# Top-k attention with a leaky-ReLU MLP: the weights of the last units of five chunks transposed on TensorE

## The chip, the cores and the metric

The kernel runs on one core of a Trainium2 chip. The metric is device time in microseconds (us): the median of three runs is 1514.51 us, and they lie between 1513.94 and 1515.4. The profile is of one further execution, with a span of 1512.7 us from the first to the last instruction.

Names of the engines in the profile: PE is TensorE (PEld its loading of weights), DVE is VectorE, ACT is ScalarE, POOL is GpSimd, SP is SyncE, which issues the DMAs.

## What is computed

An attention that keeps 32 scores of each row, and then an MLP with a leaky ReLU:

```python
# q, k, v: (8, 8, 576, 64) float32
scores = scale * np.matmul(q, k.transpose(0, 1, 3, 2))
kth = np.partition(scores, -32, axis=-1)[..., -32:-32 + 1]
scores = np.where(scores >= kth, scores, -1000000000.0)
scores = scores - np.max(scores, axis=-1, keepdims=True)
attn = np.exp(scores)
attn = attn / (np.sum(attn, axis=-1, keepdims=True) + 1e-09)
o = np.matmul(attn, v)
# (B, H, S, D) -> (B*S, H*D): 4608 tokens of 512
x = o.transpose(0, 2, 1, 3).reshape(4608, 512)
h = x @ w_in                      # w_in (512, 2048)
g = np.maximum(0.01 * h, h)
out = g @ w_out                   # w_out (2048, 512)
```

## The kernel before

The weights of the MLP come as 64-bit numbers in 16 pieces and are rounded to float32 on the chip in a first stage of some 80 us. Then the kernel works through 144 units. A unit is 128 query rows of a pair of heads, and step s does parts of several units: the top-k of unit s on VectorE, the mask of unit s-1 on GpSimd and its exponents on ScalarE, and the normalizing and transposing of unit s-2. In even steps come the scores of two units and the products with the values of two units. Tokens are gathered in chunks, two of 128 and then 17 of 256; when all units of a chunk have their values, the MLP of the chunk may run, and its matmuls are dealt out over the following steps.

The program's order on each engine is that of this code; nothing is reordered. Each engine takes its instructions one after the other.

Rounding a piece (cut to what the change touches):

```python
nc.vector.tensor_scalar(scale, scale, 1151.0, 896.0, ALU.min, ALU.max)
if n % 2:
    nc.scalar.activation(scale, scale, AF.Copy, bias=-896.0 * 128, scale=128.0)     # L127
nc.vector.tensor_scalar(m_top, top, 0xF, 0x3F80, ALU.bitwise_and, ALU.bitwise_or)   # L128
nc.vector.tensor_scalar(top, top, 0x8000, None, ALU.bitwise_and)
if n % 2 == 0:
    nc.vector.tensor_scalar(scale, scale, 896.0, 128.0, ALU.subtract, ALU.mult)     # L131
# ... sums on TensorE into pw (in PSUM), then
nc.vector.tensor_tensor(scale, scale, top, ALU.bitwise_or)                          # L144
nc.vector.tensor_tensor(dst[:, at], pw, scale[:, at].bitcast(BF16), ALU.mult)       # L147
```

The parts of a unit's way that matter here:

```python
def exponents(u, i):                                   # L238
    nc.scalar.activation(u.s[i], u.s[i], AF.Exp, bias=u.nbias[:, i:i + 1], scale=SCALE,
                         accum_out=u.z[:, i:i + 1])

def sums(u):                                           # L243
    u.ze = small.tile([P, 2], F32, name="ze")
    nc.scalar.activation(u.ze, u.z, AF.Copy, bias=1e-9, scale=1.0)

def reciprocals(u):                                    # L247
    u.rz = small.tile([P, 2], F32, name="rz")
    nc.vector.reciprocal(u.rz, u.ze)

def normalize(u, i):                                   # L250
    nc.scalar.activation(u.s[i], u.s[i], AF.Copy, bias=0.0, scale=u.rz[:, i:i + 1])

def transpose(u):
    pairs = u.both.rearrange("p i n -> p (i n)").bitcast(U16).rearrange("p (n h) -> p n h", h=2)
    apart = halves.tile([P, 2, 2 * S], U16, name="apart")          # in DRAM
    for h in range(2):
        split = work.tile([P, 2 * S], U16, name="split", bufs=2)
        nc.scalar.copy(split, pairs[:, :, h])                      # L259
        nc.sync.dma_start(apart[:, h, :], split)
    u.wT = work.tile([P, 2 * NKC - 1, P], F32, name="wT", bufs=3)
    nc.sync.dma_start_transpose(out=u.wT.bitcast(U16), in_=apart.rearrange("p h n -> (p h) n"))
```

The budget that deals out the MLP. A step has seven slots; mlp_steps(budget) puts so many columns of matmul into the order, and the budget of a slot is what is left of the work that is ready, divided by the slots until the next chunk is ready:

```python
def values_at(n):
    return n + LAG + (n + LAG) % 2                     # LAG = 3: always an even step

def attended(s):
    for at, ch in ready_at:
        if at == s:
            ready.append(ch)
            backlog[0] += mlp_cost(ch)

def slot_budget(s):
    after = [at for at, _ in ready_at if at >= s]
    until = after[0] if after else s
    few = len(after) >= len(CHUNKS) - EARLY            # EARLY = 2
    return backlog[0] / (max(until + 1 - few - s, 1) * SLOTS)      # SLOTS = 7
```

And one step:

```python
cur, old, older = unit(s), unit(s - 1), unit(s - 2)
budget = slot_budget(s)
slot()                                 # a quarter of the top-k of cur, on VectorE
mask(old, 0); mask(old, 1)
mlp_steps(budget)
slot()
reciprocals(older); normalize(older, 0); normalize(older, 1)
mlp_steps(budget)
exponents(old, 0)
transpose(older)
slot()
mlp_steps(budget); mlp_steps(budget)
slot()
mlp_steps(budget)
exponents(old, 1)
sums(old)
# even steps: scores of one unit, values of two units, attended(s), scores of another
budget = slot_budget(s + 1)
mlp_steps(budget); mlp_steps(budget)
load_more(s)
```

The matmuls of the MLP are ph (first layer, L308 for the two small chunks and L333 for the others), evacuated by ScalarE into gT through the leaky ReLU (L313 and L339), and pz (second layer, L345). The small chunks have their activations transposed on TensorE (pt, L318, copied by L320). The scores are psc (L198), copied to s_sb (L207); the values are po (L283), copied to x (L297).

Of the kernel before, what the change touches and what calls it, by code (L numbers as in the profile page):

```python
# [8 lines left out]
F32 = mybir.dt.float32  # L9
# [4 lines left out]
ALU = mybir.AluOpType  # L14

NKC = 5
# [3 lines left out]
def kernel(  # L20
# [13 lines left out]
    nc = tc.nc  # L34
    NPAIR, P, S = qT.shape
# [24 lines left out]
    work = ctx.enter_context(tc.tile_pool(name="work", bufs=2))  # L60
# [3 lines left out]
    ps_po = ctx.enter_context(tc.tile_pool(name="ps_po", bufs=1, space=bass.MemoryType.PSUM))  # L64
    ps_ml = ctx.enter_context(tc.tile_pool(name="ps_ml", bufs=3, space=bass.MemoryType.PSUM))

    ident = const.tile([P, P], F32, name="ident")
# [12 lines left out]
    NPIECE = 2 * HP * DFF // WCH  # L80
# [3 lines left out]
    def piece(n):  # L84

        if n < NPIECE // 2:
            j, c = divmod(n, HP)
            return w_in[c][:, j * WCH:(j + 1) * WCH]
        f = 2 * (n - NPIECE // 2)
        return w_out[f // 4][:, f % 4:f % 4 + 2, :].rearrange("p g n -> p (g n)")  # L90
# [12 lines left out]
    def round_weights(n):  # L103

        raw = raw_of.pop(n)
        dst = piece(n)  # L110
        mid = raw[:, :, 2]
        low = raw.rearrange("p n w -> p (n w)").bitcast(U32).rearrange("p (n w) -> p n w", w=2)[:, :, 0]
        top = raws.tile([P, WCH], U16, name="top", bufs=2)
        scale = raws.tile([P, WCH], U16, name="scale", bufs=2)
        parts = work.tile([P, 2 * NKC - 1, P], F32, name="wT", bufs=3)
        parts = parts.rearrange("p c n -> p (c n)").bitcast(U16)
        m_top, m_low = parts[:, 0:WCH], parts[:, WCH:2 * WCH].bitcast(BF16)
        nc.scalar.copy(top, raw[:, :, 3])
        nc.scalar.activation(dst, mid, AF.Copy, bias=-7.0 - 2.0 ** -16, scale=2.0 ** -20)

        nc.scalar.activation(m_low, low, AF.Copy, bias=128.0, scale=2.0 ** -29)  # L121
        yield
        nc.vector.tensor_scalar(scale, top, 4, 0x7FF, ALU.logical_shift_right, ALU.bitwise_and)

        nc.vector.tensor_scalar(scale, scale, 1151.0, 896.0, ALU.min, ALU.max)
        if n % 2:
            nc.scalar.activation(scale, scale, AF.Copy, bias=-896.0 * 128, scale=128.0)  # L127
        nc.vector.tensor_scalar(m_top, top, 0xF, 0x3F80, ALU.bitwise_and, ALU.bitwise_or)  # L128
        nc.vector.tensor_scalar(top, top, 0x8000, None, ALU.bitwise_and)
        if n % 2 == 0:  # L130
            nc.vector.tensor_scalar(scale, scale, 896.0, 128.0, ALU.subtract, ALU.mult)  # L131
        if n < NPIECE - 3:
            pw = ps_sc.tile([P, 2, 512], F32, name=f"psc{n % 2}")
            sums = [(pw[:, h, :], h * 512) for h in range(2)]
            ends = [(pw.rearrange("p h n -> p (h n)"), 0)]
        else:
            ends = sums = [(ps_ml.tile([P, 512], F32, name="pw", tag="ml"), h * 512) for h in range(2)]
        for pw, c in sums:
            at = slice(c, c + 512)
            nc.tensor.matmul(pw, ident_top, m_top[:, at].bitcast(BF16), start=True, stop=False)  # L140
            nc.tensor.matmul(pw, ident, dst[:, at], start=False, stop=False)
            nc.tensor.matmul(pw, ident_low, m_low[:, at], start=False, stop=True)
        yield
        nc.vector.tensor_tensor(scale, scale, top, ALU.bitwise_or)  # L144
        for pw, c in ends:
            at = slice(c, c + pw.shape[-1])
            nc.vector.tensor_tensor(dst[:, at], pw, scale[:, at].bitcast(BF16), ALU.mult)  # L147
# [97 lines left out]
# [8 lines that stand above are left out]
# [8 lines left out]
        u.wT = work.tile([P, 2 * NKC - 1, P], F32, name="wT", bufs=3)  # L261
        nc.sync.dma_start_transpose(out=u.wT.bitcast(U16), in_=apart.rearrange("p h n -> (p h) n"))

    x_of = {}
# [89 lines left out]
    def mlp_cost(ch):  # L356
        n = CHUNKS[ch]
        if ch < EARLY:
            return NFC * DMODEL + NFC // 4 * (HP * 512 + 2 * P)
        return NFC * HP * max(n, 225) + -(-n // P) * NFC * DMODEL  # L360
# [4 lines left out]
    def mlp_steps(budget):  # L365
        owed[0] += budget
        while owed[0] > 0:
            if running[0] is None:
                if not ready:
                    owed[0] = 0.0  # L370
                    return
                running[0] = mlp(ready.pop(0))
            cost = next(running[0], None)
            if cost is None:
                running[0] = None
            else:
                owed[0] -= cost
                backlog[0] -= cost

    LAG = 3

    def values_at(n):

        return n + LAG + (n + LAG) % 2

    steps = units

    def unit(n):  # L390
        return steps[n] if 0 <= n < len(steps) else None
# [9 lines left out]
# [10 lines that stand above are left out]
        few = len(after) >= len(CHUNKS) - EARLY  # L411
        return backlog[0] / (max(until + 1 - few - s, 1) * SLOTS)
# [3 lines left out]
    with tc.manual_schedule():  # L416
        last = {p: n for n, u in enumerate(steps) for p in u.pairs}

        def load_more(s):

            for of, load, n, lag in ((qk_of, load_qk, LOADED, -2), (v_of, load_v, LOADED_V, LAG + 1)):
                while len(of) < NPAIR and (len(of) < n or last[len(of) - n] + lag <= s):
                    load(len(of))


        for n in range(3):
            load_weights(n)
        rounding = {}
        for n in range(NPIECE + 2):
            for i in (n, n - 1, n - 2) if AS_WORDS else ():  # L430
                if 0 <= i < NPIECE:
                    if i == n:
                        rounding[i] = round_weights(i)
                    next(rounding[i], None)
            load_weights(n + 3)
            if 6 <= n < 6 + HP:
                load_qk(n - 6)
            elif n == NPIECE - 1:
                for u in steps[0:2]:
                    scores(u)  # L440
            if n == NPIECE - 1:
                load_v(0)
                load_v(1)

        for s in range(len(steps) + LAG + 1):
            cur, old, older, new = unit(s), unit(s - 1), unit(s - 2), ()
            if s % 2 == 0:
                new = [u for u in steps[s + 2:s + 4] if u]
            picks = top_k(cur) if cur else iter(())
            budget = slot_budget(s)  # L450

            def slot():
                next(picks, None)

            slot()
            if old:
                mask(old, 0)
                mask(old, 1)
            mlp_steps(budget)
            slot()  # L460
            if older:
                reciprocals(older)
                normalize(older, 0)
                normalize(older, 1)
            mlp_steps(budget)
            if old:
                exponents(old, 0)
            if older:
                transpose(older)
            slot()  # L470
            mlp_steps(budget)
# [3 lines that stand above are left out]
            if old:  # L475
                exponents(old, 1)
                sums(old)
            for u in new[:1]:
                scores(u)
            if s % 2 == 0:  # L480
                po = ps_po.tile([P, 2, P], F32, name="po")
                for values in (weigh_values, keep_values):
                    for n, u in enumerate((unit(s - LAG - 1), unit(s - LAG))):
                        if u:
                            values(u, po[:, n, :])
                attended(s)
            for u in new[1:]:
                scores(u)
            budget = slot_budget(s + 1)
# [3 lines that stand above are left out]
        mlp_steps(1e9)  # L493
# [58 lines left out]
```

## Time and profile before

| | before |
|---|---|
| time, median of 3 | 1514.51 us |
| span of the profile | 1512.7 us |
| PE busy | 1429.0 us (94%) |
| PE loading weights | 934.5 us (62%) |
| DVE busy | 1330.4 us (88%) |
| ACT busy | 1121.5 us (74%) |
| POOL busy | 1079.5 us (71%) |
| DMA of the kernel's queue | 225.49 MB, 54.2% of 16 engines |
| mean granted TensorE clock | 0.973 |

A row of a timeline has the start, the duration, the engine, the line of the kernel, the operation, what is written and read, the shape and the count of merged instructions; in brackets stands how long the engine was idle before it and what ended that. A float32 matmul of the program appears as two records in the trace, so that the 64 ph of a chunk are 128 records. Busy time of an engine that is not the bound costs nothing, and neither does its idle time; what counts is which engine is full in a stretch, and what it waits for where it is not. The matmuls are pipelined, so their durations overlap and a group's duration is read from the timeline, not from the mean.

### The profile page before, as it was taken

How to read it: one execution, taken by the hardware profiler on the slowest of the kernel's cores; microseconds unless marked ns; L12 is line 12 of the kernel's file. 1: busy time of each engine (PE TensorE's matmuls, PEld its weight loads, DVE VectorE, ACT ScalarE, POOL GpSimd, SP SyncE). 2: the span in 40 equal slices, each digit the busy share in tenths (PEclk: the TensorE clock that was granted, in tenths of full speed). 3: DMA queues.
4: the chain of work that ended last, by engine and by line, in shares of the span. 5: the costliest groups of instructions: out<-in, count | busy, mean ns of one | idle time of the engine just before them, and what ended most of it. 6: DMA issues, size and time to landing. Idle time of an engine off the chain costs nothing.

```text
span 1512.7 us, 24128 instructions
## 1 busy us (share of the span) xinstructions
PE 1429.0 (94%) x8030; PEld 934.5 (62%) x8032; DVE 1330.4 (88%) x3421; ACT 1121.5 (74%) x2149; POOL 1079.5 (71%) x726
## 2 busy tenths in 40 slices
PE   5736988999999999999999999999999999999998
PEld 2314545767676766676767676767666766666774
DVE  6899899999999999899999998999999989999600
ACT  7846887878787877787878787878787777787720
POOL 0058788887878777778787787878887878788700
PEclk9965999999999999999999999999999999999999
DMA  7714466655655556656664565645755555555510
GB/s 283 282 31 125 119 169 182 161 139 143 186 154 151 128 164 158 174 126 156 173 169 137 141 159 168 171 132 149 186 157 150 134 158 154 151 140 136 140 52 14
DMA packets 399293, 227.03 MB, mean 150 GB/s; under 512 B 343360, under 2 KB 343360, under 8 KB 397120
## 3 DMA queue, kind: packets, MB, share of 16 engines
q1 hardware_dynamic: 399168, 225.49, 54.2%
q8 instruction: 63, 1.03, 0.3%
q14 instruction: 62, 0.51, 0.1%
HBM read 46.14 MB, written 94.37 MB: 93 GB/s over the span
## 4 chain that ended last, share of the span: by engine, by line
PE 84%; DVE 10%; ACT 3%; DMA 2%; issue 1%; SPq 0%; DVEq 0%; ACTq 0%
PE pz L345 31%; PE ph L333 31%; PE psc L198 10%; PE po L283 10%; DVE tops L221 4%; DVE pairs L224 3%; DMA wT<-apart 1%; DVE pairs L216 1%; PE ph L308 1%; DVE scale L144 1%; ACT split L259 1%; ACT scale L127 0%; ACT wT L121 0%; DVE w_in L147 0%; ACT s_sb L238 0%
## 5 line engine op out<-in xcount | busy, mean ns | idle before, releaser
L234 POOL TENSOR_SCALAR pen<-s_sb,tops 128x576 f32<-128x576 f32 x288 | 638.4, 2217 | 234.8 <-DVE tops L221 205.9
L221 DVE MAX8 tops<-pairs 128x8 f32<-128x288 f32 (+1 forms) x1152 | 635.8, 591 | 0.0
L345 PE MATMUL pz<-w_out,gT 128*128 128x512 f32 x1152 | 506.7, 595 | 0.0
L333 PE MATMUL ph<-x,w_in 128*128 128x256 f32 x2176 | 482.4, 381 | 0.0
L224 DVE MATCH_REPLACE8 pairs<-tops,pairs 128x288 f32<-128x288 f32 (+1 forms) x864 | 460.0, 537 | 0.0
L333 PEld LDWEIGHTS ph<-x,w_in 128*128 128x128 f32 x2176 | 408.9, 190 | 77.1 <-issue 19.8
L235 POOL TENSOR_TENSOR s_sb<-s_sb,pen 128x576 f32<-128x576 f32 x288 | 406.9, 1413 | 24.0
L345 PEld LDWEIGHTS pz<-w_out,gT 128*128 128x128 f32 x1152 | 215.9, 190 | 264.4 <-issue 263.5
L259 ACT COPY split<-s_sb 128x1152 uint16<-128x1152 uint16 x288 | 315.7, 1144 | 0.0
L207 ACT COPY s_sb<-psc 128x576 f32<-128x576 f32 x288 | 169.4, 639 | 108.9 <-PE psc L198 108.9
L250 ACT ACTIVATE s_sb<-s_sb,rz 128x576 f32<-128x576 f32 x288 | 206.7, 767 | 33.0 <-DVE rz L247 33.0
L238 ACT ACTIVATE s_sb<-s_sb,nbias 128x576 f32<-128x576 f32 x288 | 221.4, 769 | 11.5 <-POOL s_sb L235 11.5
L198 PE MATMUL psc<-kt,qt 64*128 64x288 f32 (+1 forms) x1280 | 198.5, 438 | 29.3 <-ACT s_sb L207 29.1
L216 DVE TENSOR_TENSOR pairs<-s_sb 128x576 f32<-128x576 f32 x288 | 213.7, 780 | 10.2 <-ACT split L259 0.5
L283 PE MATMUL po<-wT,vt 128*64 128x128 f32 (+1 forms) x3200 | 182.7, 271 | 22.7 <-DMA wT<-apart 22.7
L283 PEld LDWEIGHTS po<-wT,vt 128*64 128x64 f32 x3200 | 163.2, 140 | 54.7 <-issue 26.9
L198 PEld LDWEIGHTS psc<-kt,qt 64*128 64x128 f32 (+1 forms) x1280 | 110.9, 180 | 102.2 <-ACT s_sb L207 38.8
L339 ACT ACTIVATE gT<-ph 128x256 f32<-128x256 f32 x272 | 99.0, 380 | 94.6 <-PE ph L333 94.3
L232 POOL TENSOR_SCALAR nbias<-tops 128x2 f32<-128x2 f32 x144 | 33.5, 233 | 92.5 <-DVE tops L221 79.7
L247 DVE RECIPROCAL rz<-ze 128x2 f32<-128x2 f32 x144 | 22.4, 155 | 72.0 <-ACT ze L243 71.4
L297 ACT COPY x<-po 128x128 f32<-128x128 f32 (+1 forms) x160 | 32.5, 264 | 60.0 <-PE po L283 59.7
L224 DVE MATCH_VALUE_LOAD pairs<-tops,pairs 128x8 f32 x864 | 62.2, 72 | 0.0
(44 smaller groups left out, 378.3 us busy)
## 6 DMA issues: line engine op xcount, KB each, us to landing
apart<-split SPq DMA_DIRECT2D x288, 288.0 KB, 2.1
raw<-in_weights_dram SPq DMA_DIRECT2D x16, 1024.0 KB, 5.3
vt<-in_vk_dram SPq DMA_DIRECT2D x32, 320.0 KB, 3.6
qt<-in_qT_dram SPq DMA_DIRECT2D x32, 288.0 KB, 3.6
kt<-in_kT_dram SPq DMA_DIRECT2D x32, 288.0 KB, 4.1
out_dram<-o_sb SPq DMA_DIRECT2D x36, 256.0 KB, 2.0
wT<-apart SPq DMA_TRANSPOSE x144, 4.6
```

What stands on the lines that cost most here:

```text
L198: nc.tensor.matmul(ps[i][r0:r0 + u.rows, half, 0:HS], qt[d, u.q0:u.q0 + u.rows], kt[d, half * HS:(half + 1) * HS], start=True, stop=True,)
L216: nc.vector.tensor_tensor(pairs[:, :, n, :], u.both[:, :, 0:HS], u.both[:, :, HS:S], op)
L221: nc.vector.max(out=u.tops[:, i, r, :], in_=rest[i])
L224: nc.vector.match_replace(out=rest[i], in_to_replace=u.tops[:, i, r, :], in_values=rest[i], imm_value=LOWEST)
L234: nc.gpsimd.tensor_scalar(pen, u.s[i], u.tops[:, i, ROUNDS - 1, 7:8], MASKED, ALU.is_lt, ALU.mult)
L235: nc.gpsimd.tensor_tensor(u.s[i], u.s[i], pen, ALU.add)
L238: nc.scalar.activation(u.s[i], u.s[i], AF.Exp, bias=u.nbias[:, i:i + 1], scale=SCALE, accum_out=u.z[:, i:i + 1])
L250: nc.scalar.activation(u.s[i], u.s[i], AF.Copy, bias=0.0, scale=u.rz[:, i:i + 1])
L259: nc.scalar.copy(split, pairs[:, :, h])
L283: nc.tensor.matmul(po[side * D:(side + 1) * D, o, :], vt[:, c, side, :], u.wT[:, c + side * NKC if c + 1 < NKC else c, r:r + n], start=(c ...
L333: nc.tensor.matmul(ph[:, 0:n], w_in[c][:, f * P:(f + 1) * P], x[c][:, 0:n], start=(c == 0), stop=(c == HP - 1),)
L345: nc.tensor.matmul(pz[0:m, 0:DMODEL], gT[f][:, r0:r0 + m], w_out[f // 4][:, f % 4, :], start=(f == 0), stop=(f == NFC - 1),)
```

## The change

It has two parts.

For the last pair of units of the first five chunks, the normalized weights are transposed on TensorE, into PSUM, and copied to SBUF by ScalarE, where the kernel before splits them into 16-bit halves, writes these to DRAM and reads them back through a transposing DMA. The values of the pair are then taken in the odd step, two steps after the top-k of the second unit, near the step's start and not at the end of the step after. It is for the stretch in which TensorE waits for a chunk to become ready.

In the rounding of the last of the 16 pieces, the scaling of the exponents goes from ScalarE to VectorE, so that it does not wait behind copies of scores. (For the even pieces the same operation moves two instructions ahead on VectorE.)

```diff
-        if n % 2:
+        if n % 2 and n + 1 < NPIECE:
             nc.scalar.activation(scale, scale, AF.Copy, bias=-896.0 * 128, scale=128.0)
+        else:
+            nc.vector.tensor_scalar(scale, scale, 896.0, 128.0, ALU.subtract, ALU.mult)
...
-        if n % 2 == 0:
-            nc.vector.tensor_scalar(scale, scale, 896.0, 128.0, ALU.subtract, ALU.mult)
...
+    def transpose_in_haste(u):
+
+        u.wT = work.tile([P, 2 * NKC - 1, P], F32, name="wT", bufs=3)
+        both = u.both.rearrange("p i n -> p (i n)")
+        for c0 in range(0, 2 * NKC - 1, 4):
+            c1 = min(c0 + 4, 2 * NKC - 1)
+            pt = ps_ml.tile([P, 4, P], F32, name="pt", tag="ml")
+            for c in range(c0, c1):
+                nc.tensor.transpose(pt[:, c - c0, :], both[:, c * P:(c + 1) * P], ident)
+            nc.scalar.copy(u.wT[:, c0:c1, :], pt[:, 0:c1 - c0, :])
...
+    HURRIED = {3, 7, 15, 23, 31}
 
     def values_at(n):
 
-        return n + LAG + (n + LAG) % 2
+        return n + LAG + (n + LAG) % 2 - ((n | 1) in HURRIED)
...
+        def values(s):
+            due = [u for n, u in enumerate(steps) if values_at(n) == s]
+            po = ps_po.tile([P, 2, P], F32, name="po") if due else None
+            for part in (weigh_values, keep_values):
+                for n, u in enumerate(due):
+                    part(u, po[:, n, :])
+            attended(s)
...
+            if s - 2 in HURRIED:
+                reciprocals(older)
+                normalize(older, 0)
+                normalize(older, 1)
+                transpose_in_haste(older)
+                older = None
             slot()
             if old:
                 mask(old, 0)
                 mask(old, 1)
             mlp_steps(budget)
+            if s - 2 in HURRIED:
+                values(s)
+                budget = slot_budget(s)
             slot()
...
-            if older:
+            if older and s - 1 not in HURRIED:
                 transpose(older)
...
             for u in new[:1]:
                 scores(u)
             if s % 2 == 0:
-                po = ps_po.tile([P, 2, P], F32, name="po")
-                for values in (weigh_values, keep_values):
-                    for n, u in enumerate((unit(s - LAG - 1), unit(s - LAG))):
-                        if u:
-                            values(u, po[:, n, :])
-                attended(s)
+                values(s)
+            if s - 1 in HURRIED:
+                transpose_in_haste(older)
             for u in new[1:]:
                 scores(u)
             budget = slot_budget(s + 1)
```

## The prediction

> **What bounds the kernel now.** I read the page first (TensorE busy 94% of the span, VectorE 88%), then the busy time of each engine in stretches of one regime each, then the engines' timelines inside them. The stretches, in us from the start; the columns are the length, then busy time and instructions of PE, PEld, DVE, ACT and POOL, the granted clock, the share of the DMA engines and GB/s:
>
> ```profile
> 114.07:122.87 8.80, 2.33 (x22) 1.93 (x20) 8.76 (x24) 5.62 (x10) 7.42 (x6) 0.50 0.51 136
> 187.70:261.20 73.50, 61.73 (x360) 36.02 (x360) 72.51 (x189) 61.09 (x125) 61.08 (x43) 0.91 0.64 173
> 332.17:407.42 75.25, 75.25 (x417) 50.70 (x416) 70.65 (x184) 58.28 (x115) 59.94 (x41) 1.00 0.60 164
> 407.42:482.79 75.37, 75.37 (x417) 50.80 (x416) 70.66 (x185) 58.40 (x115) 59.93 (x41) 1.00 0.56 152
> ```
>
> Up to about 256 us VectorE is the bound (72.51 of 73.50 us busy) and TensorE has holes. After it TensorE is never idle: a cycle of eight steps, which is one chunk of 256 tokens, takes 75.3 us, of which VectorE is busy 70.7. So both regimes are nearly full on VectorE: a step costs it 8.86 us (steps 12 to 17 start at 189.96 and 234.22 in its timeline), and TensorE's cycle is only 75.3 - 70.9 = 4.4 us longer than eight such steps. **VectorE can hardly catch up on lost time anywhere.**
>
> What makes VectorE lose time is one small instruction a step. In the order of time, ScalarE and then VectorE:
>
> ```profile
> 152.82 0.60 ACT L313 ACTIVATE scale<-ph 128x512 f32<-128x512 f32 x1 [1.51 <-PE ph L308]
> ...
> 156.17 0.77 ACT L320 COPY gT<-pt 128x128 f32<-128x128 f32 x4
> 156.80 0.81 ACT L238 ACTIVATE s_sb<-s_sb,nbias 128x576 f32<-128x576 f32 x1
> 157.48 0.23 ACT L238 ACTIVATION_READ_ACCUMULATOR s_sb<-s_sb,nbias 128x1 f32 x1
> 157.73 0.20 ACT L243 ACTIVATE ze<-z 128x2 f32<-128x2 f32 x1
> ```
>
> ```profile
> 157.97 0.17 DVE L247 RECIPROCAL rz<-ze 128x2 f32<-128x2 f32 x1 [3.83 <-ACT ze L243]
> ```
>
> The reader is to see a chain: the MLP's matmuls (ph), their evacuation on ScalarE, behind it in ScalarE's queue the second exponent and the sum ze of a unit, and VectorE's reciprocal behind that. A 0.17 us reciprocal held VectorE 3.83 us because MLP evacuations stood ahead of ze. Over the whole kernel this wait is 71.4 us in 44 pieces, 5.5 at most.
>
> The hole that the change aims at is the wait for the weights' transposition by DMA at the end of a chunk, on TensorE:
>
> ```profile
> 251.95 2.40 PE L283 MATMUL po<-wT,vt 128*64 128x128 f32 x20 [5.17 <-DMA wT<-apart]
> 254.28 1.96 PE L198 MATMUL psc<-kt,qt 64*128 64x288 f32 x8
> 256.17 13.24 PE L333 MATMUL ph<-x,w_in 128*128 128x256 f32 x60
> ```
>
> **What the Trainium skill says.** "Perfetto Trace Analysis", Sequencer Loop: an engine instruction goes into its engine's queue and waits there for its semaphores; I take from it that what stands behind it waits too. The trace agrees (the 3.83 us above). "TensorE: Matmul & The Clock Gate", Part 4: a transpose lands in PSUM, needs a copy after it, and took about 275 ns in a kernel; here the MLP's transposes have a mean of 276 ns, four of them 0.60 us together. The same page, Part 1: TensorE falls to half clock when idle; here the clock is 0.50 at 114 to 123 us, and eight score records take 2.83 us where they take 1.24 later. "Perfetto Trace Analysis", Optimization Strategy: regimes with different bounds gain from being interleaved. The kernel before does that; I find below that the change undoes it in five places.
>
> **The change, part by part.** (Units are numbered from 0; chunks 0 to 4 end with units 3, 7, 15, 23, 31, and their hurried steps are 5, 9, 17, 25, 33.)
>
> *Last piece's exponents.* VectorE waited 2.53 us for that ScalarE operation (L127, 1.07 us). It now does it itself in 0.42 us. But the product after it also needs TensorE's sums, whose second half ends at 77.74 us; 0.1 and one product of 0.69 put its end at 78.5 instead of 78.8. Gain 0.3 us.
>
> *Transposes.* Removed for ten units: two split copies (2.19 us on ScalarE) and a DMA way of about 9 us (unit 3: split at 130.15, values at 139.16). Added: 9 transposes, about 1.1 us of TensorE at full clock, and three copies, about 1.3 us of ScalarE. That is 11 us more TensorE work, all beside idle time, as will be seen, and ScalarE is eased.
>
> *Values one step earlier.* They now come early in the odd step, not at the end of the next one, some 1.7 steps or 15 us sooner. Part is lost at once: at the end of step 4, ScalarE must still copy unit 7's scores, which stand behind the transposes of unit 2, before it normalizes unit 3. With half-clock durations I get: values of unit 1 end at 124.0 (their DMA is unchanged), transposes of unit 2 at 126.2, scores of unit 7 at 129.0, their copy 129.8, normalizing (two of 0.77) 131.2, transposes 133.4 and copies 134.2, two units of values 139.0. The first ph starts at about 139.1 instead of 145.15. In later steps, at higher clock, the same queue gives **12 us from the step's start to the first ph**.
>
> *The budget, which the diff shows only in one line.* After the early values, slot_budget(s) is taken anew, for a chunk whose ready step is s itself. The next ready step it finds is therefore s, the number of steps left is max(s+1-s, 1) = 1 (the subtraction for the first chunks changes nothing), and the budget is 1/7 of the whole chunk, where the kernel before took slot_budget(s+1) and spread the chunk over 3 to 8 steps (1/21 to 1/56 a slot). Four such slots stand before exponents(old, 1) and sums(old). The built program's order confirms it: in step 17 all 64 ph matmuls stand in one block on TensorE, and all 16 evacuations before ze of unit 16 on ScalarE. So ze waits for the chunk's whole first layer, and VectorE's reciprocal, in the second slot of the next step, waits with it.
>
> *The stall.* Sizes: the first layer of a small chunk took from 145.15 to 162.0 with its transposes, 16.7 us; with the last copies, exponent and ze 18.7. That of a 256-token chunk is 128 records in 27.8 us (the tail's row at 1453.66); with the last evacuation (0.4), exponent (0.9) and ze (0.2) 29.3; in steps 25 and 33 two pz matmuls of the chunk before stand between the values and the first ph and add 1.7 (two take four records, and 32 records take 14.0), so 31.0. VectorE comes to the reciprocal 8.86 + 4.4 = 13.3 us after the hurried step's start. Its wait is the way from the step's start to the first ph, plus the layer, less 13.3:
>
> - step 5: 16.6 + 18.7 - 13.3 = 22.0
> - step 9: 12 + 18.7 - 13.3 = 17.4
> - step 17: 12 + 29.3 - 13.3 = 28.0
> - steps 25 and 33: 12 + 31.0 - 13.3 = 29.7 each
>
> Sum 126.8 us. What is left of each chunk is 3/7 of its MLP, 24 us in eight steps, and with 2.65 us of scores and values a step TensorE needs under 6 us of each 8.86: these steps run at VectorE's pace, so nothing is given back.
>
> *What the kernel before loses in the same stretch.* From step 5 (122.87) to step 43 (473.85) it takes 351.0 us for 38 steps that cost VectorE 336.7: 14.3 us of delays that the new order has in another form. And at step 43 its TensorE is behind VectorE: chunk 5's first ph comes at 482.15, 8.3 after the step's start, where an unburdened TensorE needs 3.9 (252.30 to 256.17): 4.4 us more.
>
> *Sum.* 126.8 - 14.3 - 4.4 - 0.3 = 107.8 us. From chunk 5 on both programs have the same order and TensorE is the bound, so it stays: 1514.5 + 107.8 = **1622 us**.
>
> **Rivals.** (a) *The intended gain.* If ze did not matter, the hole at 210 to 256 us (11.7 us of idle TensorE) and some of that before 145 would be filled, less 11 us of transposes: 1500 to 1510 us. The waits for the transposed weights (22.7 us on TensorE in all) speak for it; the order speaks against. (b) *TensorE remains the bound throughout, and the burst only moves work.* Then time is TensorE's work plus its idle time, 1510 to 1525. It would need VectorE to run far ahead during a burst; but the reciprocal stops it 13.3 us after the step's start, against bursts of 35 us and more. (c) *The stall is there but shorter*, with a way of 8 us in place of 12 and a quick first layer: five times 4 us less, 1602. (d) *Clock.* TensorE, loaded to two thirds between bursts, may enter each at half clock: up to 3 us each, 1637. The DMA transposes that vanish (10 of 144) are no rival: only their waits at chunk ends counted.
>
> **Range and chances.** (c) and (d) give 1602 to 1642. Only if the order of ScalarE's queue does not bind could the time stay within 2% (under 1545): 0.03. Faster by 2% would need more than all of the idle time named in (a): 0.01.
>
> **What would show it.** VectorE's wait for ze (71.4 us) should grow to 160 to 200, with five waits of 15 to 30 us; the reciprocal of unit 16 comes near 310 us. TensorE's busy share falls to about 89%, busy time up by 11 us, with the holes between 150 and 590 us. Chunk 5 starts near 590 and the rest is shifted whole. I am wrong if those five waits are short, if TensorE stays full from 250 us on, or if the steps after a burst run below VectorE's 8.86 us or well above it.

## The result, and the profile after

The changed kernel takes 1618.8 us (median of 4 runs, 1618.34 to 1619.45), the kernel before 1514.95 us in the same comparison: a ratio of 1.0685, with a 95% interval of 1.0666 to 1.0703. The span of the profile is 1616.9 us, against 1512.7.

The stretches from the last step before the change to the end, in the same columns as those of the kernel before (length, then busy time and instructions of PE, PEld, DVE, ACT and POOL, clock, DMA share, GB/s):

```profile
114.07:122.87 8.80, 2.45 (x24) 2.04 (x22) 8.80 (x25) 5.53 (x13) 7.40 (x6) 0.69 0.49 136
122.87:260.00 137.13, 109.87 (x566) 62.44 (x563) 108.31 (x284) 86.88 (x193) 92.28 (x62) 0.87 0.31 87
260.00:370.00 110.00, 92.68 (x566) 63.31 (x566) 79.97 (x208) 63.23 (x130) 67.61 (x47) 0.88 0.29 84
370.00:480.00 110.00, 94.06 (x487) 63.12 (x484) 71.80 (x190) 60.04 (x121) 63.55 (x43) 0.92 0.32 94
480.00:590.00 110.00, 89.08 (x425) 57.13 (x424) 85.32 (x220) 69.45 (x133) 69.63 (x47) 0.88 0.42 114
590.00:1616.00 1026.00, 1021.52 (x5874) 686.23 (x5872) 882.28 (x2299) 755.13 (x1484) 753.11 (x503) 1.00 0.53 144
```

In 122.87 to 590 us neither VectorE nor TensorE is full: in each of the stretches of 110 us VectorE stands idle for 25 to 38 us and TensorE for 16 to 21. That is the picture of two engines that work in turns. From 590 us on the kernel is as it was.

VectorE's reciprocals that waited long, from its timeline; each is the reciprocal of the unit whose sum ze stood behind a chunk's first layer:

```profile
151.75 0.17 DVE L247 RECIPROCAL rz<-ze 128x2 f32<-128x2 f32 x1 [15.71 <-ACT ze L243]
199.59 0.17 DVE L247 RECIPROCAL rz<-ze 128x2 f32<-128x2 f32 x1 [12.35 <-ACT ze L243]
299.29 0.17 DVE L247 RECIPROCAL rz<-ze 128x2 f32<-128x2 f32 x1 [28.77 <-ACT ze L243]
402.22 0.17 DVE L247 RECIPROCAL rz<-ze 128x2 f32<-128x2 f32 x1 [30.93 <-ACT ze L243]
503.98 0.17 DVE L247 RECIPROCAL rz<-ze 128x2 f32<-128x2 f32 x1 [30.14 <-ACT ze L243]
```

Five waits, 117.9 us together. What ScalarE did before the third of them, the end of step 17:

```profile
294.44 0.38 ACT L350 ACTIVATE gT<-ph 128x256 f32<-128x256 f32 x1 [1.34 <-PE ph L344]
296.16 0.38 ACT L350 ACTIVATE gT<-ph 128x256 f32<-128x256 f32 x1 [1.34 <-PE ph L344]
297.89 0.38 ACT L350 ACTIVATE gT<-ph 128x256 f32<-128x256 f32 x1 [1.34 <-PE ph L344]
298.17 0.77 ACT L238 ACTIVATE s_sb<-s_sb,nbias 128x576 f32<-128x576 f32 x1
298.83 0.19 ACT L238 ACTIVATION_READ_ACCUMULATOR s_sb<-s_sb,nbias 128x1 f32 x1
299.06 0.20 ACT L243 ACTIVATE ze<-z 128x2 f32<-128x2 f32 x1
```

ScalarE is nearly idle here (1.34 us before each evacuation of 0.38, waiting for TensorE), and the exponent at 298.17 waits for nothing but its turn: GpSimd had written the last mask of its unit by 264.05 us (262.65 + 1.40).

```profile
262.65 1.40 POOL L235 TENSOR_TENSOR s_sb<-s_sb,pen 128x576 f32<-128x576 f32 x1
```

TensorE meanwhile ran the first layer in one piece:

```profile
269.96 27.89 PE L344 MATMUL ph<-x,w_in 128*128 128x256 f32 x128
297.69 7.03 PE L356 MATMUL pz<-w_out,gT 128*128 128x512 f32 x16
```

In the list of waits (engine, line, waited for: us in total, times, longest) the row of the reciprocal reads, before and after:

```profile
DVE rz L247 <- ACT ze L243: 71.4, 44, 5.5
```

```profile
DVE rz L247 <- ACT ze L243: 177.5, 47, 30.9
```

It grew by 106.1 us, and the span by 104.2.

### The profile page after: what moved, and what is told of

Read it like the earlier page. It is cut to its first block, busy times and chain, and to the rows that moved or that the text cites. A ratio compares the mean times of both kernels' runs of the same rounds, so it can differ in the third digit from the quotient of the medians.

```text
span 1616.9 us, 24298 instructions
## 1 busy us (share of the span) xinstructions
PE 1470.4 (91%) x8122; PEld 961.8 (59%) x8122; DVE 1331.6 (82%) x3422; ACT 1117.4 (69%) x2158; POOL 1077.8 (67%) x726
## 4 chain that ended last, share of the span: by engine, by line
PE 77%; DVE 11%; ACT 5%; DMA 5%; issue 1%; SPq 0%; DVEq 0%; ACTq 0%
PE ph L344 29%; PE pz L356 26%; PE po L294 9%; PE psc L198 9%; DVE tops L221 5%; DVE pairs L224 4%; DMA wT<-apart 3%; PE ph L319 2%; ACT split L259 1%; DVE pairs L216 1%; ACT s_sb L250 1%; PE pt L272 1%; ACT s_sb L238 1%; DMA apart<-split 1%; DMA raw<-in_weights_dram 1%
## 5 line engine op out<-in xcount | busy, mean ns | idle before, releaser
L356 PE MATMUL pz<-w_out,gT 128*128 128x512 f32 x1152 | 522.7, 609 | 0.0
L356 PEld LDWEIGHTS pz<-w_out,gT 128*128 128x128 f32 x1152 | 221.1, 196 | 273.1 <-issue 272.3
L259 ACT COPY split<-s_sb 128x1152 uint16<-128x1152 uint16 x268 | 293.7, 1144 | 0.0
L294 PE MATMUL po<-wT,vt 128*64 128x128 f32 (+1 forms) x3200 | 191.1, 277 | 60.6 <-DMA wT<-apart 60.6
L198 PE MATMUL psc<-kt,qt 64*128 64x288 f32 (+1 forms) x1280 | 206.2, 450 | 43.0 <-ACT s_sb L207 42.3
L294 PEld LDWEIGHTS po<-wT,vt 128*64 128x64 f32 x3200 | 169.2, 145 | 94.2 <-DMA wT<-apart 52.2
L198 PEld LDWEIGHTS psc<-kt,qt 64*128 64x128 f32 (+1 forms) x1280 | 114.3, 185 | 122.6 <-ACT s_sb L207 53.7
L247 DVE RECIPROCAL rz<-ze 128x2 f32<-128x2 f32 x144 | 22.3, 155 | 177.8 <-ACT ze L243 177.5
```

The costliest lines, as they stand in the source:

```text
L198: nc.tensor.matmul(ps[i][r0:r0 + u.rows, half, 0:HS], qt[d, u.q0:u.q0 + u.rows], kt[d, half * HS:(half + 1) * HS], start=True, stop=True,)
L294: nc.tensor.matmul(po[side * D:(side + 1) * D, o, :], vt[:, c, side, :], u.wT[:, c + side * NKC if c + 1 < NKC else c, r:r + n], start=(c ...
L356: nc.tensor.matmul(pz[0:m, 0:DMODEL], gT[f][:, r0:r0 + m], w_out[f // 4][:, f % 4, :], start=(f == 0), stop=(f == NFC - 1),)
```

## The experiments

The theory: the change is slow because the budget taken anew puts 4/7 of a chunk's MLP ahead of ze in ScalarE's order, and VectorE stands at the reciprocal until then. The first rival: the transposes on TensorE and the early values cost the time themselves. The second: TensorE as such is overloaded during the burst, whatever stands where.

The kernels of this section, each against the kernel before on the same chip (whose median was between 1513.85 and 1514.95 us). "Wait for ze" is the row shown above, from each kernel's list of waits; the last column is where the first ph of chunk 5 starts, from which on all the kernels have the same order. The last three columns come from one profiled execution of each kernel, whose time lies up to 3.0 us from the kernel's median, so that differences of 2 or 3 us between them say little.

| kernel | median us | ratio, 95% interval | span us | wait for ze us | chunk 5 at |
|---|---|---|---|---|---|
| before | | | 1512.7 | 71.4 | 482.15 |
| changed | 1618.8 | 1.0685 [1.0666, 1.0703] | 1616.9 | 177.5 | 586.64 |
| 1 budget spread | 1529.2 | 1.0094 [1.0079, 1.0109] | 1524.6 | 85.1 | 498.48 |
| 2 burst alone | 1583.84 | 1.0457 [1.0443, 1.0472] | 1579.8 | 139.2 | 549.41 |
| 3 sum first | 1603.93 | 1.0595 [1.058, 1.0609] | 1601.6 | 162.2 | 570.61 |
| 4 half burst | 1567.54 | 1.0345 [1.0329, 1.0361] | 1568.8 | 127.8 | 539.97 |
| 5 spread, sum first | 1528.35 | 1.0095 [1.0082, 1.0108] | 1526.6 | 85.5 | 500.05 |
| 6 as 5, three chunks | 1526.58 | 1.0086 [1.007, 1.0101] | 1525.8 | 84.2 | 498.85 |
| 7 as 5, one chunk | 1518.39 | 1.0026 [1.0016, 1.0036] | 1518.7 | 79.7 | 489.87 |
| 8 last piece alone | 1514.96 | 1.0007 [0.9999, 1.0015] | 1516.0 | 75.1 | 485.62 |
| 9 one chunk, old deadlines | 1513.27 | 0.9991 [0.9984, 0.9997] | 1509.6 | 70.5 | 480.10 |
| 10 five chunks, old deadlines | 1530.49 | 1.0108 [1.0092, 1.0123] | 1526.9 | 86.2 | 497.73 |
| 11 transposes alone | 1525.43 | 1.0075 [1.0061, 1.0089] | 1523.0 | 82.2 | 494.18 |

In every row the wait for ze has grown by the same as the span, within 2.3 us. VectorE's own work is the same in all (1330.1 to 1332.2 us busy), and between the first stage and the last steps its reciprocal is nearly the only place where it stops; so this row measures the loss, in whichever engine it arises, and a cause has to be shown by the edits.

**1. The budget spread.** The changed kernel with

```diff
-                budget = slot_budget(s)
+                budget = slot_budget(s + 1)
```

> The changed kernel with one edit: after the early values the budget is slot_budget(s + 1), so that a chunk is spread over the steps until the next chunk, as in the kernel before. Theory (the burst ahead of the sums ze holds VectorE's reciprocal): the five waits of 12 to 31 us go, some 118 us, and the time falls to 1505 to 1518 us, my estimate 1510. Rival (TensorE's transposes and the early values cost the time themselves): most of the 104 us stays, 1560 or more.

Measured 1529.2 us: 89.6 of the 104 us are gone with one term of one line, so the burst is the cause of six sevenths of the loss and the first rival falls for that part. But I expected 1510, and 15 us remain.

**2. The burst alone,** in the kernel before, with its transposes by DMA and its values in even steps:

```diff
             mlp_steps(budget)
+            if s - 1 in (6, 10, 18, 26, 34):
+                budget = backlog[0] / SLOTS
             slot()
```

> The kernel before with the burst alone: transposes by DMA and values in even steps as before, but in the step after a chunk of the first five gets ready four slots take 1/7 of the whole backlog each. Theory: ze waits for the chunk's whole first layer again. Here the first ph comes about 4 us after the step's start, so that the five waits come out shorter than in the changed kernel: about 10, 12, 20, 22 and 22 us; less the 14.3 us of delays that they replace and 4.4 us of TensorE's lag, 67 us: 1582 us, between 1565 and 1600. Rival (the transposes or early values are the cost): 1515 to 1525.

Measured 1583.84 us. The five waits are 9.81, 11.27, 20.25, 19.78 and 20.98 us, where 10, 12, 20, 22 and 22 were expected. The burst needs neither the transposes nor the early values to cost 70 us; with them it costs 35 us more, because the hurried step's way to the first ph is longer, and the wait with it. The five ways are 4.0 to 5.0 us here and 7.7 to 15.5 in the changed kernel, 38.5 us more in all, and the five waits are 35.8 us longer.

**3. The sum first.** The changed kernel, burst and all, with the exponents and the sum of the unit before moved:

```diff
                 values(s)
+                exponents(old, 0)
+                exponents(old, 1)
+                sums(old)
                 budget = slot_budget(s)
```

(and left out at their old places in these steps).

> The changed kernel with the same burst on TensorE, but in the five hurried steps the exponents and the sum ze of the unit before go into ScalarE's order ahead of the burst's evacuations. Theory of the order of ScalarE's queue: the reciprocal of that unit no longer waits; the next unit's does, one step of 8.86 us later, because its normalizing, exponents and ze (5.5 us) stand behind the same evacuations. Each stall shrinks by about 4.5 us: 22 us in all, 1597 us (1590 to 1603). Rival (VectorE waits because TensorE as such is overloaded for 35 us, whatever stands where on ScalarE): no change, 1616 to 1622.

Measured 1603.93 us, 15 us less than the changed kernel where 22 were expected, and 0.9 us above the range; TensorE's order is untouched. The five long waits fell from 117.9 to 92.1 us (10.94, 11.00, 22.24, 23.95, 23.95), and they are now those of the next unit, as expected. At chunk 2:

```profile
267.99 0.17 DVE L247 RECIPROCAL rz<-ze 128x2 f32<-128x2 f32 x1 [2.27 <-ACT ze L243]
299.18 0.17 DVE L247 RECIPROCAL rz<-ze 128x2 f32<-128x2 f32 x1 [22.24 <-ACT ze L243]
```

Of the saving, 2.27 to 3.32 us came back at the later chunks as waits at the moved sum, which still stood behind the copies of the values. The second rival, no change, falls: it matters where ze stands in ScalarE's queue.

**4. Half the burst.**

```diff
-                budget = slot_budget(s)
+                budget = slot_budget(s) / 2
```

> The changed kernel with half the burst: slot_budget(s) / 2 after the early values, so that about 9 of the 16 evacuations stand ahead of ze. Theory: a wait is the way to the first ph plus the layer's part ahead of ze less 13.3 us; with the ways of the changed kernel's trace (11.1, 8, 12.9, 15.6, 14.5) and half-bursts of about 11 (small chunks) and 17.5 us: 8.8, 5.7, 17.1, 19.8 and 18.7, in sum 70 in place of 118, so 1571 us (1560 to 1582). Rival (the size of the burst does not matter, only that the chunk is taken early): 1616 to 1622.

Measured 1567.54 us. The five waits are 7.68, 14.74, 15.85, 16.16 and 14.73, in sum 69.2 where 70 was expected. That the sum agrees is partly luck: the second, of a small chunk, was expected at 5.7, the last two at 19.8 and 18.7. Full, half and spread give 1618.8, 1567.5 and 1529.2: the loss follows the size of what stands ahead of ze.

**5 and 6. What is left after the spread.** My second theory was that ze stood behind the way to the first ph in the hurried steps themselves. Kernel 5 is kernel 1 with the exponents and the sum ahead of values(s); kernel 6 is the same with HURRIED = {3, 7, 15}.

> The changed kernel with the chunk spread (slot_budget(s + 1)), and in the five hurried steps the exponents and the sum ze of the unit before ahead of the early values in ScalarE's order. Theory (what is left of the loss with the spread budget is again ze, behind the way to the first ph of 9 to 16 us): the waits in the hurried steps (4.66, 4.01, 2.76, 5.72, 3.23 us with the spread alone, 20.4 in all) shrink to under 1 us each, some of it returns at the next unit: 1515 us (1508 to 1522). Rival (the transposes and copies themselves cost it): as with the spread alone, 1526 to 1532.

> The same with only the first three chunks hurried. Theory: for the fourth and fifth chunk TensorE is full already, so that their transposes (about 2.2 us a pair and some 1.4 us of holes each) are a pure loss: 6 to 8 us below the version with five, about 1508 us (1502 to 1515). Rival (the late chunks' hurry is free or gains): equal to or above the version with five.

Measured 1528.35 and 1526.58 us. The theory falls: the sum in front gains nothing (wait for ze 85.5 against 85.1), the waits only turn up one unit later, and leaving out two of the five chunks gains less than the intervals can tell, where 6 to 8 us were expected.

**7. One chunk.** As 5, with HURRIED = {15}.

> The same with only the third chunk hurried, the one before which TensorE has most idle time. Theory: its first ph comes about 13 us after step 17's start, near 247 us in place of 256, but the next chunk is ready when it was before, so that at most the 4.4 us by which TensorE lags VectorE at a chunk's start can be gained: 1511 us (1508 to 1516). Rival (filling the hole of 5 to 12 us counts in full): 1503 to 1507.

Measured 1518.39 us, slower than before by 0.16 to 0.36% where a gain of 3 us was expected: the theory and its rival both miss. The first ph of chunk 2 came only at 254.00 us (256.17 before): step 17 started at 239.22 instead of 234.22, after waits for ze of 1.11 and 2.58 us that the kernel before does not have there. (Another 1.5 us of it is a longer wait in step 8, 5.37 in place of 3.83, before any step that this edit touches; kernel 8 shows it too.)

**8. The last piece alone,** the first hunk of the change in the kernel before:

> The kernel before with the second part of the change alone, the last piece's exponents scaled on VectorE. Theory: the top-k starts 0.3 us sooner, since TensorE's sums end then anyway: 1513.8 to 1514.5, no difference that can be measured. Rival (the 2.53 us wait counts in full): 1511.5 to 1512.5.

Measured 1514.96 us, 0.5 us above the expected range, with an interval of the ratio that contains 1. In VectorE's timeline the 2.53 us wait is gone, and two new ones, for TensorE's sums, stand in its place:

```profile
74.73 0.68 DVE L144 TENSOR_TENSOR scale<-scale,top 128x1024 uint16<-128x1024 uint16 x1
76.63 0.69 DVE L147 TENSOR_TENSOR w_out<-pw,scale 128x512 f32<-128x512 f32 x1 [1.22 <-PE pw L142]
77.87 0.69 DVE L147 TENSOR_TENSOR w_out<-pw,scale 128x512 f32<-128x512 f32 x1 [0.54 <-PE pw L142]
78.47 1.42 DVE L216 TENSOR_TENSOR pairs<-s_sb 128x576 f32<-128x576 f32 x2
```

The top-k starts at 78.47 in place of 78.80. That is not a gain that can be told from chance: in the eleven profiled kernels that have this edit it starts at 78.15 to 79.11, in the two that don't at 78.80 and 78.89.

**9 and 10. The deadlines.** An early chunk also has an earlier ready step, and slot_budget crowds the chunk before it into fewer steps. Kernel 9 hurries one chunk, kernel 10 five; both spread the budget and reckon with the even steps of the kernel before (the exponents stay in their old places; taken is the set of the chunks whose MLP is already being dealt out):

```diff
-        after = [at for at, _ in ready_at if at >= s]
+        after = [at + (at % 2) for at, ch in ready_at if ch not in taken]
...
-                budget = slot_budget(s)
+                budget = slot_budget(s + 1)
```

> Only the third chunk hurried, the budget after the early values spread, and every chunk's budget still reckoned to the even step in which its successor was ready before, so that the second chunk is spread over as many steps as in the kernel before. Theory (an earlier deadline crowds the chunk before it, and its evacuations make ze late: waits of 1.11 and 2.58 us before step 17 with one chunk hurried): these go, 1514 us (1511 to 1517). Rival (the hurried step itself costs the 4.5 us): 1517 to 1520.

> All five chunks hurried, the budget spread, and each reckoned to the even step as in the kernel before. Theory of the crowding: the waits for ze between steps 5 and 43 fall below the 33 us of the version with the spread budget alone, 1519 us (1513 to 1525). Rival (the hurried steps' own scores, transposes and copies): as with the spread budget alone, 1526 to 1532.

Kernel 9: 1513.27 us against 1514.30, ratio 0.9991 with an interval of 0.9984 to 0.9997. It is the only one of the eleven versions whose interval lies below 1, and it does so by 0.03 to 0.16%, which is too little to build on. The waits before step 17 are gone, as expected (the exponents' place differs from kernel 7's as well, so the two are not one edit apart). On TensorE its third chunk begins so, and its fourth:

```profile
247.29 6.21 PE L344 MATMUL ph<-x,w_in 128*128 128x256 f32 x28
...
330.93 12.25 PE L344 MATMUL ph<-x,w_in 128*128 128x256 f32 x56
```

8.9 us earlier than before at chunk 2 (247.29 against 256.17), and 0.5 us at chunk 3 (330.93 against 331.42). The early start is given back within one chunk: the next one is ready in step 26, when VectorE's top-k has made it ready, and VectorE's steps do not come sooner (step 26 starts at 315.52 us, before at 314.44).

Kernel 10: 1530.49 us, no better than kernel 1, where 1519 was expected. For five chunks the crowding is not the cause of the rest.

**11. The transposes alone:** TensorE transposes the ten units, but their values come in the even step and the budget is as before:

```diff
-        return n + LAG + (n + LAG) % 2 - ((n | 1) in HURRIED)
+        return n + LAG + (n + LAG) % 2
...
-            if s - 2 in HURRIED:
-                values(s)
-                budget = slot_budget(s)
```

> The first half of the change alone: the ten units' weights transposed on TensorE, but their values in the even step and the budget as before. Theory: some 2 us of TensorE a pair, of which only the pairs of the fourth and fifth chunk lie in the stretch in which TensorE is full, less some 5 us of waits for the transposed weights before chunk 2: 1513 to 1519, my estimate 1516. Rival (the transposes on TensorE are what makes the hurried versions slow): 1525 or more.

Measured 1525.43 us, 11 us slower than before. I had 1516 and the rival 1525: here the rival is right, the transposes and their place in the order cost 11 us by themselves. The first ph of chunks 2, 3, 4 and 5 come at 260.00, 340.44, 418.82 and 494.18 us, in the kernel before at 256.17, 331.42, 406.79 and 482.15: 3.8 us are lost up to chunk 2, then 5.2, 3.0 and nothing. The 3.0 is one pair's transposes in a full stretch of TensorE:

```profile
394.19 1.09 PE L272 MATMUL pt<-ident,s_sb 128*128 128x128 f32 x8
395.52 0.33 PE L272 MATMUL pt<-ident,s_sb 128*128 128x128 f32 x1 [0.24 <-ACT wT L273]
395.78 1.24 PE L198 MATMUL psc<-kt,qt 64*128 64x288 f32 x8
396.95 3.70 PE L356 MATMUL pz<-w_out,gT 128*128 128x512 f32 x8
400.49 1.12 PE L272 MATMUL pt<-ident,s_sb 128*128 128x128 f32 x8
401.76 0.33 PE L272 MATMUL pt<-ident,s_sb 128*128 128x128 f32 x1 [0.15 <-ACT wT L273]
401.93 10.47 PE L356 MATMUL pz<-w_out,gT 128*128 128x512 f32 x24
```

From 394.19 to 395.78 and from 400.49 to 401.93 make 3.0 us, where I had 2.2. The ninth transpose waits for a PSUM buffer that ScalarE has to empty. Of the 5.2 us between chunks 2 and 3, the pair's transposes take the same 3.0 (315.81 to 317.39 and 322.10 to 323.55), and the first 60 ph records of chunk 2 another 2.2:

```profile
260.00 15.40 PE L344 MATMUL ph<-x,w_in 128*128 128x256 f32 x60
```

In the kernel before they took 13.24 us (256.17). The granted clock was 0.86 in these 15.40 us and 1.00 in those 13.24; why it was lower was not tried. The 3.8 us up to chunk 2 may be chance in part: kernel 8, which has no transposes on TensorE for these units, starts chunk 2 at 257.75 in its profiled execution, 1.6 us late. Kernel 11 has a wait of 3.53 us before step 9, at the reciprocal that now stands first in the hurried steps.

That these 11 us are the same as the 15 that the spread left over is not shown. Kernel 1 starts its chunks 2 to 5 1.6, 6.7, 11.1 and 16.3 us late; 5.3 us of that arise between chunks 4 and 5, where kernel 11 loses nothing. With the burst gone, then, the transposes can cost most of the rest, but how the rest of kernel 1 is made up stays open.

## Why the prediction was right

The predicted time was 1622 us, the measured 1618.8. That only 3 us lie between them is partly luck: single terms miss by up to 8.9 us, in both directions. By its steps:

- **Both regimes are nearly full on VectorE, so that it cannot catch up.** Right. After a burst it ran at its own pace (steps 35 and 43 start at 508.28 and 579.20 us, 8.87 us a step), with TensorE busy 51.27 of these 70.92 us.
- **The burst, and the stall that follows from it.** Right in kind and place, shown by kernels 1, 2 and 4; that it acts through ScalarE's order is shown by kernel 3. The five waits are 12.35 to 30.93 us, where 15 to 30 were forecast; the reciprocal of unit 16 comes at 299.29, not near 310, since the two waits before it were 11 us shorter than reckoned. From the first ph to the reciprocal it took 18.1 us for both small chunks and 29.3, 29.2 and 29.2 for the large ones, where 18.7 and 29.3 were predicted (in the 31.0 of the last two, 1.7 are the two pz, which are counted with the way here). The 18.7 rests on a slip: from 145.15 to 162.0 are 16.9 us, not 16.7.
- **The way to the first ph** is the term that was mis-sized: 11.1, 7.7, 12.9, 15.5 and 14.4 us, where 16.6, 12, 12, and (with the two pz) 13.7 twice were predicted. For the first I reckoned scores at half clock, 2.83 us; the clock was 0.69 in 114 to 123 us where it had been 0.50, and the scores of unit 7, now behind transposes, took 1.24; two units of values, reckoned at 4.8 us, took 3.01. For the last two, two pz matmuls ahead of the values stood in the way too (2.35 us in step 25), which the prediction does not count. Together the waits are 117.9 us in place of 126.8.
- **TensorE's lag at step 43.** Predicted 3.9 us from the step's start to chunk 5's first ph, measured 7.4 (579.20 to 586.64):

```profile
577.33 2.40 PE L294 MATMUL po<-wT,vt 128*64 128x128 f32 x20 [6.25 <-DMA wT<-apart]
580.99 2.82 PE L198 MATMUL psc<-kt,qt 64*128 64x288 f32 x8 [1.26 <-ACT s_sb L207]
583.74 3.06 PE L356 MATMUL pz<-w_out,gT 128*128 128x512 f32 x4
586.64 12.27 PE L344 MATMUL ph<-x,w_in 128*128 128x256 f32 x56
```

  The 6.25 us are not the reason: the values end 0.5 us after the step's start, in the stretch that the 3.9 was taken from (252.30 to 256.17) 2.0 after it. What was left out comes behind them, a wait of 1.26 us and scores of 2.82 (1.96 there), and four pz records of 3.06 us that do not stand there. So 586.64 in place of 589.9: 8.9 us less from the waits, 3.5 more here, and 2.1 more elsewhere, of which 1.2 are two small waits for ze.
- **TensorE's busy time.** Predicted 11 us more and a share of 89%, measured 41.4 more (1470.4) and 91%. The step that failed is the assumption that the rest of its work keeps its duration: between the bursts the clock was 0.84 to 0.86, and twelve pz records took 5.42 us at 511.76 (clock 1.00 in 508 to 519 us) and 7.49 at 530.54 (0.70 in 530 to 538). The time did not depend on it, since TensorE was not the bound there.
- **The last piece.** Predicted 0.3 us. The top-k starts at 78.49 in the changed kernel, 0.3 us sooner, but kernel 8 and the spread of these starts leave the gain unshown. It is too small to matter.
- **The transposes "all beside idle time".** Wrong for this code: with the burst taken away they and their order cost 11 us. What they cost in the changed kernel was not measured; those of a hurried pair lie on the way to the first ph there, and so inside the waits.
- **The rivals.** (a) and (b) put the time at 1525 us or less, and fall. For (c), one of the five ways was as short as 8 us (7.7, step 9). (d) did not come about where it was looked for: in 269.96 to 297.80 and 474.75 to 502.40 us, two of the bursts, the clock was 1.00. The upper end of the range, 1642, is 5 us above what (d) comes to; no term of the prediction stands for these.

## What to carry to other kernels

Where a program's order is fixed, look for the small instruction through which two engines are tied, and count what stands ahead of it in each queue: a 0.2 us sum behind 28 us of evacuations stopped the engine that was nearly the bound. A budget that is spread "until the next deadline" becomes a burst when it is asked for at the deadline itself, so print the order of the built program, not only the diff. And starting one stage earlier gains only what the next stage can use: kernel 9 began a chunk 8.9 us earlier and kept about 1 us of it in the median (2 us at chunk 5 of the profiled execution).

## What the runs showed that I had not expected

The granted clock of a lightly loaded stretch was not fixed by the order of TensorE's instructions. In 114 to 123 us it was 0.50 in the kernel before, 0.50 in kernels 2 and 9 and 0.69 in kernels 7 and 8, though TensorE has the same work there in all five; in all five the scores that follow took 2.82 to 2.83 us. In the changed kernel and in kernels 1 and 11, which put nine transposes ahead of these scores, they took 1.24. These are readings of one execution each, and what sets the clock in such a stretch was not tried. And nine transposes of 128x128 float32 in a row, 272 ns each in the trace, take about 1.45 to 1.6 us with one wait for a PSUM buffer: a sixth of a microsecond each, so that the mean duration of a record says little of what a row of them costs.
